# Attention and feed-forward on one core: partition sums split over two steps, and the softmax reciprocal placed behind the next maximum

## The chip, the cores and the metric

The kernel runs on one core of one Trainium2 chip. The metric is the device time of one execution in microseconds (us). The times shown are medians of several executions. One further execution was recorded with the hardware profiler; all times inside the kernel come from that one.

## What is computed

The reference is an attention with mixing across heads, followed by a feed-forward layer. Cut to what matters:

```
B, H, S, D = 4, 12, 448, 64
scores = (q @ k^T) / sqrt(D)                  # per batch and head
scores = einsum('bhij,hg->bgij', scores, w_pre)
attn   = softmax(scores, axis=-1)
attn   = einsum('bhij,hg->bgij', attn, w_post)
x      = (attn @ v) as [B*S, 768]
h      = x @ w_in                             # 768 -> 2048
out    = (h * sigmoid(1.702 h)) @ w_out       # 2048 -> 768
```

## The kernel before

**Steps.** Attention is cut into 180 steps: four batches, and 45 groups of ten query rows (the last has eight) in each. Ten rows by twelve heads make 120 partitions, so one step's scores are a tile of 120x448. The main loop runs over the step `i`, and what it emits is, engine by engine, the order in which the engines work; no scheduler reorders it. In step `i` it emits, in this order:

- the gather of the scores of step `i+4` from HBM (SyncE's queue, SP), into one of four buffers `r`;
- `mix(i+1)` on TensorE: the product with the first mixing matrix, into one of two PSUM buffers `mx`;
- for batch 0, `post_whole(i-2)` (the second mixing) and `keep_whole(i-3)`; for the later batches `keep_upper(i-4)` on ScalarE;
- for batch 0, `weigh_mix(i-1)` on GpSimd; for the later batches `weigh(i-1)` (GpSimd, writes `w`), `upper(i-1)` (ScalarE, writes `a`), `lower(i-1)` (GpSimd). All need the reciprocal `rs` of step `i-1`;
- `peak(i)` on VectorE (L286, the row maximum `nm`) and `expo(i)` on ScalarE (L293, the exponential `e` with its row sum `sm`, which frees the `mx` buffer). With `expo(i)` GpSimd turns the row sum into `rs` (L299);
- `run_jobs(i)`: the side jobs whose turn has come (below);
- products of the feed-forward layer (`h`, L588, and `po`, L627), 2.15 groups a step once the first batch has been through attention, `post(i-3)`, the scores of later chunks (`qk`) and the context products (`av`);
- last on VectorE, `keep_lower(i-4)` (L383) and `inverse(i)` (L304), the reciprocal of `rs`, in place.

After the last step only feed-forward products are left.

**Side jobs.** A job has a first step, the jobs that it comes after with a lag in steps, and a cost in the tokens of an engine; a job that isn't urgent waits until its engine's tokens suffice. The largest are sixteen conversions of weight slices (`convert`): fetch in three parts, five VectorE instructions a part (`w_f`, L484 to L504), a sum of squares on ScalarE (`waste`, L96), the sum over partitions and the scale, the upper part on ScalarE and the lower on VectorE (`w_p`, L532 and L537), and a store to HBM, from where the feed-forward stage fetches each slice again (`wt`). Other jobs scale q, k and v of the later batches (`tops`) and x (`gs`).

**Sums over partitions.** Each scale needs a sum over all partitions. `add_all` (L104 to L109) does it: TensorE multiplies the partial sums by a matrix of ones, into the last 16 columns of the PSUM bank `pp` that holds the newest second mixing, and VectorE adds along the row (L109). Both are emitted at the same place in the same step. There are 28 such sums: 16 for weights (`w_n`), eight for q, k and v (`tops`), four for x (`gs`).

Of the kernel before, what the change touches and what calls it, by code (L numbers as in the profile page):

```python
# [38 lines left out]
def attention_then_feed_forward(ctx, tc, q, k, v, w_pre, w_post, w_in, w_out, out):  # L39
# [63 lines left out]

    def add_all(m, parts):  # L104

        p, n = parts.shape
        t = last_pp[-1][:, 512 - 16:512 - 16 + n]
        nc.tensor.matmul(t, ones[:p, :], parts, start=True, stop=True)
        nc.vector.tensor_reduce(m, t, axis=AX.X, op=ALU.add)  # L109


# [26 lines left out]
    def top_of(name, b):  # L138
        i = 3 * b + "kqv".index(name)
        return tops[:, i:i + 1]  # L140

    def join(name, b):
        add_all(top_of(name, b), st["m" + name, b])

# [144 lines left out]
    def expo(i):  # L289
        K = rows_of(steps[i][1])[1] * H  # L290
        e = flow.tile([KG, S], F32, name=f"e_{i}", tag="e", bufs=3)
        sm = stat.tile([KG, 1], F32, name=f"sm_{i}", tag="sm")
        nc.scalar.activation(  # L293
            e[:K], row.pop(("mx", i))[:K, :S], AF.Exp, bias=row.pop(("nm", i))[:K, 0:1],
            scale=1.0, accum_out=sm[:K, 0:1],
        )
        rs = stat.tile([KG, 1], F32, name=f"rs_{i}", tag="rs")
        by = 2.0 ** -10 if steps[i][0] else 1.0
        nc.gpsimd.tensor_scalar(rs[:K], sm[:K], 1e-9, by, op0=ALU.add, op1=ALU.mult)  # L299
        row["e", i], row["rs", i] = e, rs  # L300

# [137 lines left out]

    def join_x(b):  # L440
        e = gs[:, b, 0:1]
        add_all(e, st["mx", b])

    def scale_x(b):
# [19 lines left out]
    def convert(kind, s, first):  # L464
# [45 lines left out]

        def join_w():
            t["n"] = stat.tile([128, 1], F32, name=f"{nm}_n", tag="wn")
            add_all(t["n"], t["m"])

# [31 lines left out]
        for a in range(NP):  # L546
# [11 lines left out]
            sizes.append(job(first, "A", 0.7, lambda a=a: size(a), after=[(last, 1)]))  # L558
        j = job(first, "D", 0.2, join_w, after=[(x, 1) for x in sizes])
        j = job(first, "D", 0.9, scale_w, after=[(j, 0)])  # L560
# [172 lines left out]
    for b in range(1, B):  # L733
# [6 lines left out]
        for name, first, ready in (("k", z - 25, z - 17), ("q", z - 23, z - 17), ("v", z - 8, z + LAG + 7)):  # L740
# [3 lines left out]
            for i in range(THIRDS):  # L744
# [3 lines left out]
                a["stage"][1].append(sq[-1])  # L748
            jn = job(0, "D", 0.2, lambda name=name, b=b: join(name, b), after=[(x, 1) for x in sq], urgent=True)
            sizes[name] = job(0, "D", 0.7, lambda name=name, b=b: scale(name, b), after=[jn], urgent=True)  # L750
            for i in range(THIRDS):
# [146 lines left out]
    sq = [job(1 + 2 * i, {"A": 1.6}, 0, lambda eng, i=i: squares("v", 0, i, eng, 2), urgent=True) for i in range(THIRDS)]  # L898
    j = job(1, "D", 0.2, lambda: join("v", 0), after=sq, urgent=True)
    job(1, "D", 0.9, lambda: scale("v", 0), after=[j], urgent=True)  # L900

# [50 lines left out]
    while quanta or i < N + LAG + 12:  # L952
# [15 lines left out]
        if GPB <= i - LAG - 1 < N:  # L968
            keep_upper(i - LAG - 1)
            spend("A", 0.55)  # L970
        if 0 <= i - 1 < GPB:
            weigh_mix(i - 1)
# [8 lines left out]
        if i < N:  # L981
            peak(i)
            spend("D", 0.62)
            expo(i)
            spend("A", 0.82)
        run_jobs(i)
# [13 lines left out]
        for b, c, pr in at_context.pop(i, []):  # L1000
# [7 lines left out]
            if c == NCH - 1 and pr == NPAIR - 1:  # L1008
                z = i
                a = job(z + 2, "D", 0.2, lambda b=b: join_x(b), urgent=True)  # L1010

                def finish(b=b, z=z):
                    scale_x(b)
                    x_done[b] = cur[0] + 1
                job(z + 3, "D", 0.9, finish, after=[a], urgent=True)
        slot()
# [3 lines left out]
        if GPB <= i - LAG - 1 < N:  # L1020
            keep_lower(i - LAG - 1)
            spend("D", 0.64)
        if i < N:
            inverse(i)
            spend("D", 0.15)
        owed = min(owed, 3.0)
# [44 lines left out]
```

## Time and profile before

| | us |
|---|---|
| median of 3 runs | 1029.36 |
| lowest and highest run | 1024.65, 1032.99 |
| the profiled execution | 1027.42 |
| its span in the profile | 1025.7 |

The span runs from the first to the last instruction that the profile shows; the profiled execution is 1.7 us longer than its span. Mean granted clock of TensorE over the execution: 0.961 of full speed. In the profile PE is TensorE, PEld its weight loads, DVE VectorE, ACT ScalarE, POOL GpSimd, and SP or SPq SyncE's queue of transfers. A wait is idle time of an engine, put down to the instruction that ended it.

### The profile page before, as it was taken

Reading aid. Unit: us, or ns where it says so; the run is one execution under the profiler, and the core shown is the slowest. Engines: PE = TensorE matmul, PEld = TensorE weight load, DVE = VectorE, ACT = ScalarE, POOL = GpSimd, SP = SyncE. Lnnn points to the kernel's source line nnn. Section 1 sums busy time; section 2 is a strip of 40 time slices with the busy share of each in tenths; the row PEclk is TensorE's granted clock in tenths of the full one; section 3 lists DMA queues with packets and bytes.
Section 4 is the critical chain, followed back from the end, with each engine's and each line's share of the span. In section 5 each row is a group of like instructions: output and inputs, shape, how many; then the busy total and the mean of one; then the engine's idle time right before and its main releaser. Section 6 shows DMA issues by size and latency. Waiting matters only on the chain.

```text
span 1025.7 us, 19868 instructions
## 1 busy us (share of the span) xinstructions
PE 925.0 (90%) x7344; PEld 542.4 (53%) x7344; DVE 628.8 (61%) x1389; ACT 605.2 (59%) x1380; POOL 354.5 (35%) x536
## 2 busy tenths in 40 slices
PE   5678878877899889999899999999899999999998
PEld 4345555544455444555455555656455666555554
DVE  5658786698976796554644575555645565443334
ACT  3666768677577676765657657656656564323332
POOL 0111111145433455343533454334534444001221
PEclk9888999888999998999999999999999999999999
DMA  8988979768557656654676647546654341234322
GB/s 301 289 275 313 332 267 323 259 197 245 190 198 244 232 187 181 192 172 131 202 225 207 202 150 234 166 130 179 212 164 146 108 148 64 93 123 151 118 93 85
DMA packets 66565, 198.19 MB, mean 193 GB/s; under 512 B 7668, under 2 KB 32372, under 8 KB 66468
## 3 DMA queue, kind: packets, MB, share of 16 engines
q1 hardware_dynamic: 66064, 196.83, 59.4%
q8 instruction: 58, 0.95, 0.4%
q14 instruction: 39, 0.32, 0.1%
q10 hardware_dynamic: 404, 0.09, 0.1%
HBM read 140.27 MB, written 56.62 MB: 192 GB/s over the span
## 4 chain that ended last, share of the span: by engine, by line
PE 62%; DVE 17%; ACT 8%; DMA 8%; issue 3%; POOL 1%; SPq 0%; ACTq 0%; DVEq 0%; POOLq 0%
PE po L627 19%; PE h L588 18%; PE mx L279 8%; PE av L408 4%; PE qk L243 3%; PE pp L356 2%; PE pp L358 2%; PE pp L357 2%; DVE w_p L537 2%; DMA sd<-sc 2%; ACT waste L96 2%; DVE w_f L504 2%; DMA w<-in_moe_w_out_dram 2%; DVE nm L286 2%; ACT e L293 1%
## 5 line engine op out<-in xcount | busy, mean ns | idle before, releaser
L627 PE MATMUL po<-g,wt 128*128 128x448 f16 x1152 | 243.8, 355 | 11.3 <-DVE th L609 6.8
L588 PE MATMUL h<-x,wt 128*128 128x448 f16 x1152 | 244.1, 356 | 3.9 <-ACT sc L253 2.9
L279 PE MATMUL mx<-r,wa 120*120 120x448 f32 x360 | 183.3, 592 | 40.0 <-ACT e L293 29.7
L343 POOL TENSOR_TENSOR a<-w,a 120x448 f16<-120x448 f32 x135 | 150.8, 1117 | 130.2 <-issue 71.5
L627 PEld LDWEIGHTS <-wt 128*128 128x128 f16 x1152 | 109.4, 99 | 130.0 <-issue 45.1
L588 PEld LDWEIGHTS <-wt 128*128 128x128 f16 x1152 | 109.2, 98 | 117.0 <-issue 31.2
L329 POOL TENSOR_SCALAR w<-e,rs 120x448 f32<-120x448 f32 x135 | 88.2, 653 | 227.3 <-DVE rs L304 217.8
L337 ACT ACTIVATE a<-e,rs 120x448 f16<-120x448 f32 x135 | 91.0, 674 | 106.1 <-DVE rs L304 106.1
L657 DVE SCALAR_TENSOR_TENSOR acc<-po,ct,acc 128x448 f32<-128x448 f32 x141 | 96.1, 682 | 74.3 <-PE po L627 72.2
L293 ACT ACTIVATE e<-mx,nm 120x448 f32<-120x448 f32 x180 | 113.6, 631 | 31.2 <-POOL wr L309 25.4
L609 DVE SCALAR_TENSOR_TENSOR th<-th,h 128x448 f32<-128x448 f32 x64 | 39.7, 620 | 137.8 <-ACT th L606 137.8
L606 ACT ACTIVATE th<-h,ct 128x448 f32<-128x448 f32 x64 | 40.5, 633 | 140.2 <-PE h L588 129.6
L253 ACT COPY sc<-qk 120x448 f32<-120x448 f32 (+1 forms) x186 | 89.6, 532 | 41.8 <-PE qk L233 28.9
L286 DVE TENSOR_REDUCE nm<-mx 120x1 f32<-120x448 f32 x180 | 108.9, 605 | 1.9 <-PE mx L279 1.9
L356 PE MATMUL pp<-wp,a 120*112 120x120 f16 x540 | 95.7, 220 | 14.8 <-DVE p L383 14.3
L279 PEld LDWEIGHTS mx<-r,wa 120*120 120x120 f32 x360 | 61.6, 193 | 83.9 <-ACT e L293 47.0
L299 POOL TENSOR_SCALAR rs<-sm 120x1 f32<-120x1 f32 x180 | 56.8, 315 | 115.8 <-ACT e L293 103.8
L358 PE MATMUL pp<-wp,a 120*112 120x120 f16 x540 | 95.1, 219 | 0.0
L357 PE MATMUL pp<-wp,a 120*112 120x120 f16 x540 | 94.9, 218 | 0.0
L383 DVE TENSOR_TENSOR p<-pp,p 112x480 f16<-112x480 f32 x135 | 87.2, 647 | 5.9 <-ACT p L379 5.9
L356 PEld LDWEIGHTS <-a 120*112 120x112 f16 x540 | 71.5, 132 | 26.9 <-DVE p L383 12.1
L357 PEld LDWEIGHTS <-a 120*112 120x112 f16 x540 | 71.8, 133 | 15.9 <-issue 9.5
(126 smaller groups left out, 1258.1 us busy)
## 6 DMA issues: line engine op xcount, KB each, us to landing
wt<-wd SPq DMA_DIRECT2D x64, 768.0 KB
r<-sd SPq DMA_DIRECT2D x176, 210.0 KB
sd<-sc SPq DMA_DIRECT2D x72, 420.0 KB
w<-in_moe_w_in_dram SPq DMA_DIRECT2D x24, 512.0 KB
w<-in_moe_w_out_dram SPq DMA_DIRECT2D x24, 512.0 KB
wd<-w_p SPq DMA_DIRECT2D x16, 768.0 KB
sd<-sc SPq DMA_DIRECT2D x24, 308.0 KB
out_dram<-acc SPq DMA_DIRECT2D x24, 224.0 KB
```

Source lines behind the costliest of these rows:

```text
L253: (nc.scalar.copy if engs[x] == "A" else nc.vector.tensor_copy)(t[:n, x, :], two[x][:n, :S])
L279: nc.tensor.matmul(mx[:K, :S], st["wa", b][:K, :K], row.pop(("r", i))[:K, :], start=True, stop=True)
L286: nc.vector.tensor_reduce(nm[:K], row["mx", i][:K, :S], axis=AX.X, op=ALU.max, negate=True)
L293: nc.scalar.activation(e[:K], row.pop(("mx", i))[:K, :S], AF.Exp, bias=row.pop(("nm", i))[:K, 0:1], scale=1.0, accum_out=sm[:K, 0:1],)
L337: nc.scalar.activation(a1[:K], row.pop(("e", i))[:K], AF.Copy, scale=row.pop(("rs", i))[:K, 0:1])
L343: nc.gpsimd.tensor_tensor(a2[:K], row.pop(("w", i))[:K], row["a1", i][:K], op=ALU.subtract)
L356: nc.tensor.matmul(o, a1[:K, js], wp1[:K, :, :n], start=True, stop=False)
L357: nc.tensor.matmul(o, a1[:K, js], wp2[:K, :, :n], start=False, stop=False)
L358: nc.tensor.matmul(o, a2[:K, js], wp1[:K, :, :n], start=False, stop=True)
L588: nc.tensor.matmul(h, w[:, i, c, fc * 128:(fc + 1) * 128], x[:, j, c, :], start=(n == 0), stop=(n == len(terms) - 1),)
L627: nc.tensor.matmul(po, w[:, j, fc, e * 128:(e + 1) * 128], g[:, i, fc, :], start=(n == 0), stop=(n == len(terms) - 1),)
L657: nc.vector.scalar_tensor_tensor(a, po, c, a, op0=ALU.mult, op1=ALU.add)
```

## The change

Two things are moved. First, the sums: `add_all` becomes `add_over` (TensorE's product) and `add_along` (VectorE's addition), emitted by two jobs, the second one step after the first. Both are urgent, where the weights' sum was not. The job that uses the sum now runs in the same step as the addition. Second, the reciprocal: `inverse(i)` goes from the end of step `i` to step `i+1`, right behind `peak(i+1)`. For that `peak(i)` and `expo(i)` go ahead of `weigh(i-1)`, `upper(i-1)` and `lower(i-1)`, and GpSimd's `rs` becomes a function of its own (`shifted`), emitted behind `lower(i-1)` as before.

```diff
-    def add_all(m, parts):
+    def add_over(parts):
 
         p, n = parts.shape
         t = last_pp[-1][:, 512 - 16:512 - 16 + n]
         nc.tensor.matmul(t, ones[:p, :], parts, start=True, stop=True)
+        return t
+
+    def add_along(m, t):
         nc.vector.tensor_reduce(m, t, axis=AX.X, op=ALU.add)
 
+    def sum_jobs(first, m, parts, after):
+
+        t = {}
+
+        def over():
+            t["t"] = add_over(parts())
+
+        j = job(first, None, 0, over, after=after, urgent=True)
+        return job(first, "D", 0.2, lambda: add_along(m(), t["t"]), after=[j], urgent=True)
...
-        j = job(first, "D", 0.2, join_w, after=[(x, 1) for x in sizes])
+        j = sum_jobs(first, total, lambda: t["m"], [(x, 1) for x in sizes])
         j = job(first, "D", 0.9, scale_w, after=[(j, 0)])
...
+        if i < N:
+            peak(i)
+            spend("D", 0.62)
+        if 0 <= i - 1 < N:
+            inverse(i - 1)
+            spend("D", 0.15)
+        if i < N:
+            expo(i)
+            spend("A", 0.82)
         if 0 <= i - 1 < GPB:
             weigh_mix(i - 1)
             spend("G", 0.35)
...
             lower(i - 1)
             spend("G", 1.07)
         if i < N:
-            peak(i)
-            spend("D", 0.62)
-            expo(i)
-            spend("A", 0.82)
+            shifted(i)
         run_jobs(i)
...
             keep_lower(i - LAG - 1)
             spend("D", 0.64)
-        if i < N:
-            inverse(i)
-            spend("D", 0.15)
```

The same is done for the sums of q, k, v and x.

**VectorE, steps 35 and 36, before.** `nm` is the maximum, `rs` the reciprocal, `w_n` the sum of a weight slice, and the short rows behind it the scale.

```order
L286 TENSOR_REDUCE nm_1638<-mx_1587 120x1
L109 TENSOR_REDUCE w_3_n<-pp_1630 128x1
L81 TENSOR_SCALAR w_3_n<-w_3_n 128x1
L82 TENSOR_SCALAR ew<-w_3_n 128x1
L518 TENSOR_SCALAR ew<-ew 128x1
L520 RECIPROCAL w_3_s<-ew 128x1
L521 TENSOR_SCALAR w_3_s<-w_3_s 128x1
L523 TENSOR_SCALAR ew<-ew 128x1
L304 RECIPROCAL rs_1643<-rs_1643 120x1
L286 TENSOR_REDUCE nm_1676<-mx_1628 120x1
```

The addition stands right behind the maximum of its step, and the reciprocal of the step ahead of the next maximum. The same steps in the changed kernel:

```order
L296 TENSOR_REDUCE nm_1609<-mx_1561 120x1
L319 RECIPROCAL rs_1577<-rs_1577 120x1
L112 TENSOR_REDUCE w_3_n<-pp_1563 128x1
L81 TENSOR_SCALAR w_3_n<-w_3_n 128x1
L82 TENSOR_SCALAR ew<-w_3_n 128x1
L529 TENSOR_SCALAR ew<-ew 128x1
L531 RECIPROCAL w_3_s<-ew 128x1
L532 TENSOR_SCALAR w_3_s<-w_3_s 128x1
L296 TENSOR_REDUCE nm_1645<-mx_1601 120x1
L319 RECIPROCAL rs_1617<-rs_1617 120x1
```

The reciprocal behind a maximum is now that of the step before it, and the addition reads a bank that TensorE filled a step earlier. The slice is also another one, of the first weight matrix and not of the second: the conversions have fallen behind by this place.

**VectorE in step 88, before.** `tops`, `ev` and `s_v` are the scale of v, `p` is `keep_lower`.

```order
L286 TENSOR_REDUCE nm_5150<-mx_5051 120x1
L81 TENSOR_SCALAR tops<-tops 128x1
L82 TENSOR_SCALAR ev_5157<-tops 128x1
L151 RECIPROCAL s_v_5158<-ev_5157 128x1
L152 TENSOR_SCALAR s_v_5158<-s_v_5158 128x1
L153 TENSOR_SCALAR ev_5157<-ev_5157 128x1
L156 TENSOR_SCALAR ex<-ev_5157,e_wp 128x1
L383 TENSOR_TENSOR p_3_4882<-pp_5077,p_3_4882 112x48x10
L304 RECIPROCAL rs_5155<-rs_5155 120x1
```

All conversions are over here (the last store stands in step 83). The same step in the changed kernel, from the last instruction of that scale on:

```order
L166 TENSOR_SCALAR ex<-ev_5133,e_wp 128x1
L548 SCALAR_TENSOR_TENSOR w_7_p<-w_7_f_4220,w_7_s,w_7_p 128x512
L548 SCALAR_TENSOR_TENSOR w_7_p<-w_7_f_4318,w_7_s,w_7_p 128x512
L548 SCALAR_TENSOR_TENSOR w_7_p<-w_7_f_4628,w_7_s,w_7_p 128x512
L495 TENSOR_SCALAR w_7_f_5146<-w_7_64_2_4705 128x512
L499 TENSOR_SCALAR w_7_f_5146<-w_7_f_5146 128x512
L398 TENSOR_TENSOR p_3_4844<-pp_5052,p_3_4844 112x48x10
```

Conversion work stands here that was done earlier before; the last store now stands in step 95.

**ScalarE, steps 70 and 71, before.** `e` is the exponential, `a` is `upper`, `p` is `keep_upper`.

```order
L379 CAST p_1_2936<-pp_3726 112x48x10
L337 ACTIVATE a_70_3767<-e_3704,rs_3707 120x448
L293 ACTIVATE e_3773,sm_3774<-mx_3693,nm_3771 120x448
L96 ACTIVATE waste,mq_3641<-qa_2_3646 128x448 x2
L532 ACTIVATE w_6_p<-w_6_f_2953,w_6_s 128x512
```

The upper part of step 70 stands ahead of the exponential of step 71. In the changed kernel:

```order
L394 CAST p_1_2874<-pp_3665 112x48x10
L303 ACTIVATE e_3706,sm_3707<-mx_3628,nm_3703 120x448
L352 ACTIVATE a_70_3711<-e_3634,rs_3643 120x448
L96 ACTIVATE waste,mq_3572<-qa_2_3577 128x448 x2
L96 ACTIVATE waste,w_6_m<-w_6_f_3437 128x512
```

The exponential now stands ahead of the upper part.

## Rows read from the trace of the kernel before

**Rows 1.** Busy time by stage; columns as its first line says, instructions in brackets.

```profile
core 0: us, PE busy (x) PEld busy (x) DVE busy (x) ACT busy (x) POOL busy (x), PEclk, DMA share, GB/s
34.00:195.00 161.00, 129.29 (x803) 81.16 (x802) 119.82 (x311) 117.35 (x299) 29.89 (x90) 0.92 0.88 299
195.00:258.00 63.00, 47.74 (x345) 28.75 (x345) 50.12 (x112) 40.89 (x95) 27.04 (x39) 0.83 0.70 215
258.00:414.00 156.00, 136.72 (x1073) 76.65 (x1073) 119.57 (x242) 107.62 (x243) 68.82 (x85) 0.95 0.65 212
414.00:472.00 58.00, 58.00 (x559) 34.86 (x557) 31.81 (x74) 37.80 (x88) 23.70 (x36) 1.00 0.53 160
472.00:870.00 398.00, 383.32 (x3523) 229.29 (x3521) 225.97 (x483) 245.82 (x558) 178.94 (x257) 1.00 0.54 168
```

**Rows 2.** Waits from 34 to 195 us: us in total, times, longest us.

```profile
ACT e L293 <- POOL wr L309: 25.4, 19, 3.2
PE mx L279 <- ACT e L293: 19.9, 15, 5.2
DVE rs L304 <- POOL rs L299: 17.1, 15, 3.3
DVE w_n L109 <- PE pp L108: 15.1, 8, 4.7
...
PE av L397 <- DVE x L431: 9.3, 3, 4.6
```

**Rows 3.** Timeline, parts of steps 34 to 37: start, us, instruction, in brackets the idle time before it.

```profile
158.01 0.16 DVE L304 RECIPROCAL rs<-rs 120x1 f32<-120x1 f32 x1 [0.76 <-POOL rs L299]
158.09 0.60 DVE L286 TENSOR_REDUCE nm<-mx 120x1 f32<-120x448 f32 x1
...
158.66 1.01 PE L279 MATMUL mx<-r,wa 120*120 120x448 f32 x2
...
160.65 0.16 DVE L109 TENSOR_REDUCE w_n<-pp 128x1 f32<-128x3 f32 x1 [1.95 <-PE pp L108]
...
160.89 0.65 ACT L293 ACTIVATE e<-mx,nm 120x448 f32<-120x448 f32 x1
...
166.59 0.60 DVE L286 TENSOR_REDUCE nm<-mx 120x1 f32<-120x448 f32 x1
...
167.29 0.64 ACT L293 ACTIVATE e<-mx,nm 120x448 f32<-120x448 f32 x1 [0.48 <-POOL wr L309]
```

**Rows 4.** Waits from 195 to 258 us.

```profile
DVE w_n L109 <- PE pp L108: 6.5, 3, 5.2
...
DVE rs L304 <- POOL rs L299: 3.2, 3, 1.4
```

**Rows 5.** Waits from 258 to 414 us.

```profile
DVE tops L109 <- PE pp L108: 6.8, 2, 3.4
...
DVE rs L304 <- POOL rs L299: 4.7, 5, 1.4
```

**Rows 6.** Waits from 472 to 870 us.

```profile
ACT a L337 <- DVE rs L304: 70.2, 48, 3.8
...
DVE rs L304 <- POOL rs L299: 33.7, 35, 1.4
```

**Rows 7.** Conversion instructions (tile w_f, which w_p reads): columns DVE busy, ACT busy.

```profile
0.00:1026.00 1026.00, 175.10 (x288) 65.59 (x144) 0.96 0.60 193
```

**Rows 8.** The maxima (L286), one a step, in two stretches: column DVE busy.

```profile
257.90:414.50 156.60, 15.71 (x26) 0.95 0.65 212
414.50:471.90 57.40, 7.25 (x12) 1.00 0.53 159
```

**Rows 9.** Chain of waits from 30 to 290 us: start, us, link.

```profile
49.80 9.79 DMA wd<-w_p
...
105.53 7.47 DMA r<-sd
```

**Rows 10.** A wait of the whole span.

```profile
PE pp L108 <- ACT p L379: 6.5, 7, 2.6
```

More of the change, by code (lines that the diff above doesn't have):

```diff
@@ L140, in top_of @@
         return tops[:, i:i + 1]
-    def join(name, b):
-        add_all(top_of(name, b), st["m" + name, b])
     def scale(name, b):
@@ L296, in expo, with shifted @@
         )
+        row["e", i], row["sm", i] = e, sm
+    def shifted(i):
+        K = rows_of(steps[i][1])[1] * H
+        sm = row.pop(("sm", i))
         rs = stat.tile([KG, 1], F32, name=f"rs_{i}", tag="rs")
@@ L299, in expo @@
         nc.gpsimd.tensor_scalar(rs[:K], sm[:K], 1e-9, by, op0=ALU.add, op1=ALU.mult)
-        row["e", i], row["rs", i] = e, rs
+        row["rs", i] = rs
     def inverse(i):
@@ L438, in x_size @@
                    st["mx", b][:, 2 * c + half:2 * c + half + 1], "A")
-    def join_x(b):
-        e = gs[:, b, 0:1]
-        add_all(e, st["mx", b])
     def scale_x(b):
@@ L509, in size, with total @@
             square_sum(t["f", a].bitcast(F32), t["m"][:, a:a + 1], "A")
-        def join_w():
+        def total():
             t["n"] = stat.tile([128, 1], F32, name=f"{nm}_n", tag="wn")
-            add_all(t["n"], t["m"])
+            return t["n"]
         def scale_w():
@@ L748, in attention_then_feed_forward @@
                 a["stage"][1].append(sq[-1])
-            jn = job(0, "D", 0.2, lambda name=name, b=b: join(name, b), after=[(x, 1) for x in sq], urgent=True)
-            sizes[name] = job(0, "D", 0.7, lambda name=name, b=b: scale(name, b), after=[jn], urgent=True)
+            jn = sum_jobs(0, lambda name=name, b=b: top_of(name, b), lambda name=name, b=b: st["m" + name, b], sq)
+            sizes[name] = job(0, "D", 0.7, lambda name=name, b=b: scale(name, b), after=[(jn, 0)], urgent=True)
             for i in range(THIRDS):
@@ L898, in attention_then_feed_forward @@
     sq = [job(1 + 2 * i, {"A": 1.6}, 0, lambda eng, i=i: squares("v", 0, i, eng, 2), urgent=True) for i in range(THIRDS)]
-    j = job(1, "D", 0.2, lambda: join("v", 0), after=sq, urgent=True)
-    job(1, "D", 0.9, lambda: scale("v", 0), after=[j], urgent=True)
+    j = sum_jobs(1, lambda: top_of("v", 0), lambda: st["mv", 0], sq)
+    job(1, "D", 0.9, lambda: scale("v", 0), after=[(j, 0)], urgent=True)
     at_scores = {}
@@ L1009, in attention_then_feed_forward @@
                 z = i
-                a = job(z + 2, "D", 0.2, lambda b=b: join_x(b), urgent=True)
+                a = sum_jobs(z + 2, lambda b=b: gs[:, b, 0:1], lambda b=b: st["mx", b], [])
                 def finish(b=b, z=z):
@@ L1014, in finish @@
                     x_done[b] = cur[0] + 1
-                job(z + 3, "D", 0.9, finish, after=[a], urgent=True)
+                job(z + 3, "D", 0.9, finish, after=[(a, 0)], urgent=True)
         slot()
```

## The prediction

> **What bounds the kernel now.** First the busy time by stage [rows 1], cut at the places where the kind of work changes: batch 0 (34 to 195 us, steps 0 to 44), batch 1 before any feed-forward product (to 258, steps 45 to 57), feed-forward beside conversions (to 414, steps 58 to 83), feed-forward without conversions (to 472, and on to 870); behind them the tail. From 414 on PE is the bound: busy for 58.00 of 58 and 383.32 of 398 us, and the tail is feed-forward products alone. Ahead of that it is not: it is idle for 31.7 us of the first stage (161 less 129.29), 15.3 of the second, 19.3 of the third, 66.3 in all. PE does the same products in both kernels, and the last of them end the span, so a gain is idle time of PE that goes, or a higher clock.
>
> Next, who lets PE wait in the first stage [rows 2]. 19.9 us are mixings (L279) that wait for an exponential to free a `mx` buffer, 9.3 are context products that wait for a VectorE instruction on x: 29.2 of the 31.7. The exponential in turn stood 19 times, 25.4 us in all, behind something; the row names GpSimd's `wr`, but the exponential of step 37 starts at 167.29, 0.10 us after its own maximum ends (166.59 + 0.60) [rows 3], so VectorE is what it waits for. VectorE is busy for 119.82 of 161 us, and its 41.2 us of idle time are mostly two waits: 17.1 us in 15 reciprocals that wait for GpSimd's `rs`, and 15.1 us in eight additions that wait for TensorE's product of ones. Both are waits at the head of an in-order queue. The timeline shows one of each [rows 3]: the reciprocal of step 34 waits 0.76 us and the next maximum stands behind it; 2.5 us later the addition waits 1.95 us. These are the waits that the change takes aim at.
>
> **The change, part by part.** The number of steps, the feed-forward groups in each step and the products are unchanged; nothing is added but order. PE's 28 products of ones stay where a sum is due, VectorE's additions follow a step later.
>
> *Reciprocal.* Moved behind the next maximum, `inverse(i-1)` needs an `rs` that GpSimd made most of a step earlier; a step is some 3.6 us (161 / 45), the waits were at most 3.3. I count all of them as gone from VectorE: 17.1 us in the first stage, 3.2 in the second [rows 4], 4.7 in the third [rows 5]. In return each maximum now stands ahead of the reciprocal, so `upper` and `weigh` of the step before start about 0.6 us later (a maximum takes 0.60 [rows 3]). Behind them come `lower` and, three steps on, `post`; that distance is the cover, and I cost it at nothing. Were the cover gone, 48 waits for the reciprocal in 472 to 870 [rows 6] would each be 0.6 us longer, 29 us of ScalarE, which is idle there for 152 us (398 less 245.82).
>
> *Additions.* A step after its product the addition finds it done: 15.1, 6.5 and 6.8 us go. What is late next is the maximum: it needs `mix`, which needs the exponential two steps back. Step 36's mixing runs from 158.66 to 159.67 us [rows 3], so with the addition's wait gone the next maximum could start at about 159.7, ahead of where the addition now begins (160.65); but its exponential still follows one that began at 160.89, though that one's maximum was done at 158.69: there ScalarE itself was behind. So a wait that goes is not a microsecond won each time.
>
> The sum now lies a step longer in a PSUM bank that the mixing two steps later wants. VectorE adds next behind the reciprocal, PE reaches that mixing only after the following exponential (0.65 us) and mixing (1.01 us) [rows 3]: 1.7 us of cover, cost nothing. Without it the nearest row is the opposite wait, 15.1 us in eight cases, 1.9 us each; at most ten sums of the first stage could cost that, 19 us. In the trace a product of ones waited for ScalarE's reading of the same bank seven times, 6.5 us [rows 10]. The Trainium skill (PSUM — Partial Sum Buffer, section "PSUM bank collisions raise a hardware error") says that accesses of two engines to one bank have to be kept apart by semaphores, whichever columns they touch; the trace agrees with it in those seven waits. By that rule alone this term would be a loss between 0 and the 19 us above.
>
> *Conversions.* One more step lies between a conversion's product and its scale, so each conversion takes longer and the next begins later: the last store moves from step 83 to step 95. Counted in the order, VectorE has 12 `w_f` and 3 `w_p` instructions fewer in steps 0 to 44, 5 `w_f` fewer in 45 to 57, 7 `w_f` more and 3 `w_p` fewer in 58 to 83, and 10 `w_f` and 6 `w_p` more in 84 to 95. One takes 0.61 us (175.10 / 288 [rows 7], both kinds together). That is 9.1 us less VectorE work in the first stage (15 instructions), 3.0 less in the second (5), 2.4 more in the third (4), 9.7 more in 414 to 472 (16). The fetches and stores on SP's queue move with them; the tightest is weight slice 7, stored in step 89, fetched back from step 90, used from step 93 (before: 78, 86, 93). Stores and fetches of the trace took up to 9.8 us [rows 9], and a step there is 4.8 (57.40 / 12 [rows 8]), so about 19 us for two transfers: just enough.
>
> *The sum.* First stage: VectorE loses 17.1 + 15.1 + 9.1 = 41.3 us of waits and work. Nothing of it on the path gives 0, and PE can't win more than the 29.2 us that it waits for others. ScalarE is busy for 73% (117.35 / 161), PE for 80%, the transfers for 88% of the time, so the four take turns at the end of a wait; I take a third, 14 us. Second: 3.2 + 6.5 + 3.0 = 12.7, bounds 0 and 12.7; here VectorE at 80% (50.12 / 63) is the fullest engine, so half, 6 us. Third: 4.7 + 6.8 - 2.4 = 9.1, bounds -2.4 and 9.1; I take 4 us, a bit under half, because PE's idle time there (19.3 us) has other causes too. 414 to 472: 9.7 us of work go where VectorE is idle for 26.2 (58 less 31.81), bounds: nothing lost; or the 12 steps run at the pace of the stage with conversions, 6.02 us a step (156.60 / 26) against 4.78 [rows 8], 14.9 lost. I take 4, since the added work a step (9.7 / 12 = 0.8 us) is about half of what that stage carries (65 conversion instructions in 26 steps, 1.5 us a step) and there is idle time to take it. 472 to 870: VectorE's 33.7 us of waits for `rs` go [rows 6], but PE is at work for 96%; bounds 14.7 (its idle time) and 0, I take 0. Tail: PE alone, 0. Together 14 + 6 + 4 - 4 = 20 us off the profiled execution: 1027.4 - 20 = 1007.4. That execution lies 1.9 us under the median of the runs shown, 1029.4.
>
> **The rivals.** *VectorE alone paced the early stages.* For: its idle time in the first stage is nearly all of the two kinds that go. Then PE's 29.2 us, the second stage's 12.7 and the third's 9.1 are won, 4 lost: 47.0 off, 980.4. A higher clock would help too: it was granted at 0.83 in the second stage and 1.00 from 414 on. Against: ScalarE and the transfers are nearly as full.
>
> *The gain is hidden anyway.* The chain of waits from 30 to 290 us passes through transfers, a store of 9.79 us and a gather of 7.47 among them [rows 9], and in 34 to 195 us they are busy for 0.88 of the time at 299 GB/s. If they or ScalarE set the pace, the first stage wins 3 us, the second 3, the third 0, and 2 are lost behind: 4 off, 1023.4. Against: no wait of PE in [rows 2] ends with a transfer. The Trainium skill (DMA: Bandwidth & Descriptors, section "Where 436 GB/s comes from") puts the memory's limit for one core at about 358 GB/s; by that limit (an estimate from that page) the stage's bytes would need 134 us, so that page would allow a gain of 27 us and no more.
>
> *The moved conversions starve PE (slower).* Place: steps 84 to 95, where PE has no idle time. If VectorE, with conversions back in its queue, is late for the maxima and the gates there, these 12 steps run at 6.02 us: +14.9, and with nothing won ahead, 1042.3. It decides from the point where the early stages win less than these steps lose. For: 41.5 of 58 us (31.81 + 9.7) is 72%, near the 77% (119.57 / 156) at which PE lost 19.3 us in the stage before. Against: those early stages have real waits that go.
>
> That the change doesn't do what it says (the waits stay) would need `rs` to come a whole step late; it belongs to the second rival.
>
> **How the numbers follow.** A measurement of this kernel tells about 1% from no change, 1019.1 to 1039.7. My forecast, 1007.4 with its own range of 994 to 1019, gets 0.52; the larger gain (980.4) 0.14; the hidden gain (1023.4) 0.22; the slower one (1042.3) 0.12. Faster by over 1%: 0.52 + 0.14 = 0.66; within 1%: 0.22; slower: 0.12. The range from 985 to 1033 leaves out some 0.08 of the larger gain and the slower case's 0.12.
>
> **What would show it.** Right: waits of VectorE for `rs` and for the product of ones near zero; 34 to 195 us shortened by some 14 us, the next stage by 6; steps 84 to 95 longer by a few us; 84 later steps unchanged. Wrong: VectorE's idle time in the first stage as large as before, under the name of the maximum waiting for `mix` (PE or ScalarE then set the pace); PE waits for `wt` of slice 7 around step 93; or mixings that wait for an addition in their bank.

## The result and the profile after

The changed kernel takes 1036.79 us (median of 10 runs, 1032.85 to 1039.14) where the kernel before takes 1029.86 (10 runs, 1024.65 to 1033.23): a ratio of 1.0073, 95% interval 1.005 to 1.0096. It is a little slower, where 20 us less was forecast. The profiled execution took 1032.85 us, the lowest of the ten; its span is 1031.1 us, 5.4 more than before.

The start of the maximum of a step, read from the timeline, divides both kernels at the same step. The table is worked out from these starts; the lower rows are experiments that follow.

```
us from step to step   0-44   45-57  58-83  84-95  96-178  rest
before                 196.6   61.3  156.6   57.4  392.2  161.6
after                  187.6   57.7  161.0   67.2  394.7  162.9
e1_recip_only          198.5   63.3  161.0   57.4  396.2  162.9
e2_sums_only           193.6   56.9  159.6   68.1  394.5  161.5
e3_weights_one_step    199.8   62.8  159.3   57.7  394.4  162.9
e4_cadence             199.9   59.4  155.8   57.7  393.2  162.9
e5_sums_on_time        201.4   57.6  156.4   57.7  392.8  161.6
e6_rs_ahead            198.8   57.3  155.1   57.7  393.0  163.2
e7_late_only           192.2   57.8  160.3   66.2  390.5  161.6
e8_recip_rs_ahead      199.3   61.0  158.6   57.4  393.7  163.2
e9_old_place_rs_ahead  201.7   57.9  150.9   58.0  393.9  162.4
e10_no_least           191.4   57.3  151.0   57.4  390.5  161.5
e11_more_bytes         206.5   61.4  156.7   57.4  389.7  161.7
e12_after_rs_ahead     187.1   55.0  159.5   66.8  389.2  162.9
```

"0-44" runs from the start of the span. The change wins 9.0 and 3.6 us ahead of step 58, and gives back 4.4, 9.8, 2.5 and 1.3 behind it. The 1.3 comes from the boundary chosen: from the maximum of step 178 instead of 179 on, the rest is 164.0 us before and 164.1 after. Each row is one profiled execution, and executions of one kernel lie over 8 us apart (1024.65 to 1033.23). In 96-178 the kernel before differs by 1.7 to 2.5 us from e7, e10 and e11, whose code is the same there, so differences of that size in this table mean nothing by themselves.

The products of TensorE are the same in all these kernels, so a stretch gets longer in one of two ways: TensorE idles more, or it is busy longer. The next table separates them: idle time of PE between the same steps (a stretch less its PE busy time; the first from 34 us on), the sum, PE's busy time from 34 us to step 178, the granted clock there as a share of full speed (a mean over stretches at full and at half speed), and the granted clock of whole executions, in the mean of all runs of that kernel.

```
PE idle, us            34us-44 45-57 58-83 84-95 96-177  sum   busy  clock  all runs
before                  31.7   15.2   19.3   0.0   14.7  80.9  746.8  0.960  0.962
after                   26.0   13.8   25.7   5.3   16.1  87.0  746.0  0.963  0.960
e1_recip_only           34.1   15.9   21.6   0.0   15.9  87.5  753.8  0.953  0.954
e2_sums_only            28.4   14.7   25.2   5.0   14.5  87.8  748.5  0.963  0.963
e3_weights_one_step     34.0   19.3   20.0   0.1   16.0  89.4  749.5  0.957  0.957
e4_cadence              30.6   17.1   18.1   0.1   16.2  82.1  748.8  0.961  0.958
e5_sums_on_time         32.0   14.2   15.6   0.1   14.5  76.4  753.0  0.954  0.959
e6_rs_ahead             29.8   15.1   17.0   0.1   14.5  76.5  750.1  0.957  0.960
e7_late_only            26.7   11.3   25.7   4.5   14.7  82.9  747.7  0.963  0.959
e8_recip_rs_ahead       29.6   16.1   17.9   0.0   14.1  77.7  757.2  0.949  0.953
e9_old_place_rs_ahead   31.2   14.0   16.3   0.1   14.5  76.2  750.4  0.957  0.962
e10_no_least            26.3   14.0   16.2   0.0   14.7  71.2  740.0  0.970  0.971
e11_more_bytes          37.2   15.1   19.4   0.0   13.9  85.6  749.6  0.954  0.960
e12_after_rs_ahead      26.9   11.1   24.9   5.0   14.0  81.9  740.5  0.974  0.964
```

The changed kernel idles 6.1 us more than before and is busy as long. Where the code is the same, idle time repeats within 1 us (before and e11 from step 45 on), so it tells more than the times of the first table. Busy time goes with the granted clock: 740.5 us at 0.974 in e12, 757.2 at 0.949 in e8. Why one kernel is granted less than another no run shows.

Busy time by stage of the changed kernel, between the same steps. It answers to [rows 1], and its first line names the columns.

```profile
core 0: us, PE busy (x) PEld busy (x) DVE busy (x) ACT busy (x) POOL busy (x), PEclk, DMA share, GB/s
34.00:187.60 153.60, 127.58 (x805) 79.72 (x805) 113.85 (x292) 112.32 (x288) 33.60 (x89) 0.94 0.91 304
187.60:245.30 57.70, 43.85 (x333) 26.91 (x333) 45.66 (x100) 40.20 (x96) 29.05 (x39) 0.80 0.71 216
245.30:406.20 160.90, 135.17 (x1075) 75.25 (x1075) 124.14 (x246) 105.12 (x239) 79.85 (x88) 0.97 0.66 212
406.20:473.40 67.20, 61.89 (x568) 36.59 (x567) 43.81 (x99) 46.00 (x107) 28.68 (x39) 0.98 0.51 158
```

VectorE's idle time in the first stage is 153.6 - 113.85 = 39.8 us, against 41.2 before: no less, though two kinds of waits were to go from it. What it now waits for (us in total, times, longest us), from 34 to 187.6 us, to be read against [rows 2]:

```profile
DVE w_n L112 <- ACT p L390: 12.3, 5, 3.1
DVE nm L296 <- PE mx L289: 10.3, 9, 2.9
DVE rs L319 <- POOL rs L314: 7.8, 9, 2.0
DVE tops L112 <- ACT p L390: 3.2, 1, 3.2
```

The additions (L112) waited 15.1 us for TensorE's product; now they wait 12.3 + 3.2 = 15.5 us in six cases for a ScalarE copy. The reciprocals (L319) still wait 7.8 of 17.1 us, and 10.3 us of waits of the maximum (L296) for the mixing are new. In the last attention stage, 473.4 to 868.2 us, the waits for `rs` have grown from the 33.7 us of [rows 6]:

```profile
DVE rs L319 <- POOL rs L314: 41.8, 35, 2.0
```

Why the addition waits, in the timeline of the changed kernel (start, us, instruction, idle time before it):

```profile
147.39 0.98 PE L334 MATMUL pp<-wr,e 120*112 120x120 f32 x8
...
148.21 0.29 PE L108 MATMUL pp<-w_m,ones 128*128 128x3 f32 x2
...
150.38 0.95 ACT L263 COPY sc<-qk 120x448 f32<-120x448 f32 x2
...
151.22 0.58 ACT L390 COPY p<-pp 112x480 f32<-112x480 f32 x1
...
151.83 0.16 DVE L112 TENSOR_REDUCE w_n<-pp 128x1 f32<-128x3 f32 x1 [2.87 <-ACT p L390]
```

The product of ones (L108) is done at 148.5, in the bank that holds the second mixing of 147.39. A step later `keep_whole` (L390) copies that mixing out of the bank, and the order puts it ahead of the addition. ScalarE comes to it at 151.22, behind copies of scores, and only as it ends does the addition, which reads other columns of the bank, begin. The Trainium skill (PSUM — Partial Sum Buffer, section "PSUM bank collisions raise a hardware error") has accesses of two engines to one bank kept apart, a read by ScalarE against a read by VectorE included; the trace agrees, in these six waits of 15.5 us.

Why the reciprocal waits, in the same view, steps 112 and 113:

```profile
556.01 0.61 DVE L296 TENSOR_REDUCE nm<-mx 120x1 f32<-120x448 f32 x1
...
556.72 0.63 ACT L303 ACTIVATE e<-mx,nm 120x448 f32<-120x448 f32 x1 [0.80 <-DVE rs L319]
...
557.25 0.19 ACT L303 ACTIVATION_READ_ACCUMULATOR e<-mx,nm 120x1 f32 x1
557.34 0.66 ACT L352 ACTIVATE a<-e,rs 120x448 f16<-120x448 f32 x1
...
558.13 1.04 POOL L358 TENSOR_TENSOR a<-w,a 120x448 f16<-120x448 f32 x1 [0.71 <-POOL w L344]
...
559.26 0.19 POOL L314 TENSOR_SCALAR rs<-sm 120x1 f32<-120x1 f32 x1
...
559.49 0.16 DVE L319 RECIPROCAL rs<-rs 120x1 f32<-120x1 f32 x1 [1.71 <-POOL rs L314]
```

The exponential's row sum is read out by 557.44. `rs` could be made then, but GpSimd has `lower` (L358) of the step before first in its queue, and `lower` needs `upper` (L352), which now stands behind the exponential on ScalarE. So `rs` starts 1.9 us after the exponential's end. Over steps 96 to 178 the mean from the exponential's end to the end of `rs` is 2.30 us, against 1.10 before.

### The profile page after: what moved, and what is told of

Same layout as the page of the kernel before. It is cut to its first block, busy times and chain, and to the rows that moved or that the text cites. A ratio compares the mean times of both kernels' runs of the same rounds, so it can differ in the third digit from the quotient of the medians.

```text
span 1031.1 us, 19788 instructions
## 1 busy us (share of the span) xinstructions
PE 925.2 (90%) x7344; PEld 540.1 (52%) x7344; DVE 639.4 (62%) x1386; ACT 605.2 (59%) x1383; POOL 377.0 (37%) x542
## 4 chain that ended last, share of the span: by engine, by line
PE 57%; DVE 23%; ACT 12%; issue 4%; DMA 3%; POOL 1%; SPq 0%; ACTq 0%; DVEq 0%; POOLq 0%
PE po L638 18%; PE h L599 17%; PE mx L289 7%; PE av L423 4%; DVE nm L296 3%; DVE w_p L548 2%; DVE w_f L503 2%; ACT waste L96 2%; ACT e L303 2%; PE qk L253 2%; ACT sc L263 2%; PE pp L371 2%; DVE p L398 2%; DVE w_f L499 2%; DVE w_f L509 2%
## 5 line engine op out<-in xcount | busy, mean ns | idle before, releaser
L638 PE MATMUL po<-g,wt 128*128 128x448 f16 x1152 | 248.0, 359 | 18.7 <-ACT sc L263 9.3
L303 ACT ACTIVATE e<-mx,nm 120x448 f32<-120x448 f32 x180 | 115.7, 643 | 149.2 <-DVE rs L319 143.6
L358 POOL TENSOR_TENSOR a<-w,a 120x448 f16<-120x448 f32 x135 | 149.1, 1104 | 133.0 <-issue 64.4
L344 POOL TENSOR_SCALAR w<-e,rs 120x448 f32<-120x448 f32 x135 | 112.4, 832 | 217.5 <-DVE rs L319 108.3
L668 DVE SCALAR_TENSOR_TENSOR acc<-po,ct,acc 128x448 f32<-128x448 f32 x135 | 91.9, 681 | 79.1 <-PE po L638 77.4
L296 DVE TENSOR_REDUCE nm<-mx 120x1 f32<-120x448 f32 x180 | 110.6, 615 | 13.0 <-PE mx L289 12.7
L352 ACT ACTIVATE a<-e,rs 120x448 f16<-120x448 f32 x135 | 89.9, 666 | 5.1 <-DVE rs L319 5.0
L371 PEld LDWEIGHTS <-a 120*112 120x112 f16 x540 | 71.3, 132 | 36.5 <-DVE p L398 9.6
L665 POOL TENSOR_TENSOR acc<-acc,pt 128x448 f32<-128x448 f32 x33 | 38.3, 1165 | 124.6 <-ACT pt L662 124.0
L314 POOL TENSOR_SCALAR rs<-sm 120x1 f32<-120x1 f32 x180 | 44.4, 247 | 105.8 <-ACT e L303 93.1
```

The lines of the kernel that those rows point to most:

```text
L296: nc.vector.tensor_reduce(nm[:K], row["mx", i][:K, :S], axis=AX.X, op=ALU.max, negate=True)
L303: nc.scalar.activation(e[:K], row.pop(("mx", i))[:K, :S], AF.Exp, bias=row.pop(("nm", i))[:K, 0:1], scale=1.0, accum_out=sm[:K, 0:1],)
L344: nc.gpsimd.tensor_scalar(w[:K], e[:K], row["rs", i][:K, 0:1], 1.0, op0=ALU.mult, op1=ALU.mult)
L358: nc.gpsimd.tensor_tensor(a2[:K], row.pop(("w", i))[:K], row["a1", i][:K], op=ALU.subtract)
L371: nc.tensor.matmul(o, a1[:K, js], wp1[:K, :, :n], start=True, stop=False)
L638: nc.tensor.matmul(po, w[:, j, fc, e * 128:(e + 1) * 128], g[:, i, fc, :], start=(n == 0), stop=(n == len(terms) - 1),)
```

## The experiments

Each was compared with the kernel before on the same chip, whose medians were 1028.6 to 1029.8 us. The chip was not the same for all experiments; from one to the next, the ratios compare best.

**e1, the reciprocal part alone.** The kernel before with these lines of the change and no other.

```diff
+        if i < N:
+            peak(i)
...
+        if 0 <= i - 1 < N:
+            inverse(i - 1)
...
+        if i < N:
+            expo(i)
...
-            peak(i)
...
-            expo(i)
...
+            shifted(i)
...
-        if i < N:
-            inverse(i)
```

> The reciprocal behind the next maximum alone; all sums in one step as before, so the conversions keep the schedule of before (last store in step 83). If the lateness of the conversions is what costs and the removed waits were worth something, this is faster than before by 5 to 10 us (1020 to 1025). If the early gain of the changed kernel was only conversion work moved out of the first stages, it equals before (1028 to 1032). If the new order itself costs behind step 96 (upper part behind the exponential, GpSimd's chain longer), it is slower than before by 3 to 6 us (1033 to 1036).

Measured: 1041.55 us, ratio 1.0126 (1.0099 to 1.0152). The part alone costs 12 us, more than any of the three theories had it; waits for `rs` over the whole span are 65.4 us, against 63.0 before. The conversions keep their schedule (last store in step 83), and neither the early gain nor the loss in 84-95 appears. The loss is spread over all other stages. By the second table it is 6.6 us of idle time of PE and 7.0 of longer busy time, at a lower clock (0.954 in the mean of all runs, 0.962 before).

**e2, the sums part alone.** `sum_jobs` in place of `add_all`, the reciprocal as before.

> The sums over two steps alone; the reciprocal stays at the end of its step. The conversions are late as in the changed kernel (last store in step 95). If their lateness costs, this is slower than before by 5 to 10 us (1035 to 1040), with steps 84 to 95 some 10 us longer. If the reciprocal's order is what costs, it is within 3 us of before.

Measured: 1034.89 us, 1.0049 (1.0031 to 1.0067), at the fast end of the expected loss. The early gain and the loss of 10.7 us in 84-95 are both here, and here the last store is in step 95: they belong to the sums part.

**e3, the changed kernel with the weights' sums in one step again.**

```diff
-        j = sum_jobs(first, total, lambda: t["m"], [(x, 1) for x in sizes])
+        def join_w():
+            t_ = add_over(t["m"])
+            add_along(total(), t_)
+
+        j = job(first, "D", 0.2, join_w, after=[(x, 1) for x in sizes])
```

> The changed kernel with the weights' sixteen sums in one step again; q, k, v and x keep two steps, the reciprocal stays moved. Conversions on the schedule of before. Lateness theory: steps 84 to 95 return to 57 us, total 1020 to 1026. Moved work theory: the first stages lose their 12 us again, total 1028 to 1032. Reciprocal theory: 1033 to 1036.

Measured: 1039.81 us, 1.0098 (1.007 to 1.0126). That is slower than each of the three theories had it. Conversions are back on schedule; the gain and the loss in 84-95 are both gone (57.7 us), so of the sums it is the weights' that move them. What is left is about the cost of e1, whose reciprocal part this kernel keeps.

**e4, the changed kernel with the conversions on schedule, sums split.**

```diff
-            up = job(first, "A", 0.72, lambda a=a: w_upper(a, "A"), after=[(j, 1)] + [(x, 0) for x in stores[-1:]])
+            up = job(first, "A", 0.72, lambda a=a: w_upper(a, "A"), after=[(j, 0)] + [(x, 0) for x in stores[-1:]])
```

> The changed kernel, but the upper part of a converted slice is emitted in the step of its scale and not a step later, so that the conversions keep the schedule of before (last store in step 83) though their sums take two steps. Lateness theory: 1018 to 1026, faster than before by what the additions' waits were worth. Moved work theory: 1028 to 1032. If ScalarE now waits for the scale on VectorE at the upper part, 16 such waits of 1 to 2 us: up to 1040.

Measured: 1032.45 us, 1.0029 (1.0013 to 1.0044). This is just slower than the moved-work theory had it. Sums and reciprocal stand as in the changed kernel, and steps 0-44 win nothing (199.9 against 196.6; PE idles 30.6 us there, against 31.7). VectorE waits for the mixing instead, from 34 to 195 us:

```profile
DVE nm L296 <- PE mx L289: 14.0, 11, 3.6
```

**e5, sums split and on schedule, the reciprocal in its old place.** e2 with the edit of e4.

> The sums part alone, with the conversions kept on the schedule of the kernel before (the upper half of a weight may follow its scale in the same step, so the last store falls in step 83 as before); the reciprocal stays in its old place. Theory that late conversions price the sums: the sums part alone took 1034.9, its steps 84 to 95 cost 10 us; with them back at 57.4 us and steps 0 to 57 no longer won, about 1026 to 1031, and steps 84 to 95 within 1 us of the kernel before. Theory that the addition costs by itself (it now stands behind ScalarE's copies that read the same bank): 1034 or more on this schedule too.

Measured: 1029.28 us, 0.9993 (0.9976 to 1.0009). In time the split wins nothing and loses nothing; what e2 lost comes only with late conversions. PE idles 4.5 us less than before, none of it in the first stage, but is busy longer, at a lower clock, so the split may be worth those 4.5 us; the time doesn't show it.

**e6, e4 with `rs` ahead of `lower`.**

```diff
-            lower(i - 1)
-            spend("G", 1.07)
         if i < N:
             shifted(i)
+        if GPB <= i - 1 < N:
+            lower(i - 1)
+            spend("G", 1.07)
```

> The changed kernel with conversions on schedule (1032.5) and one more edit: GpSimd makes rs of a step ahead of lower of the step before, so it no longer stands behind an instruction that waits for ScalarE's upper. Theory that the reciprocal waits because rs stands behind lower: in steps from 45 on VectorE's waits for rs fall from 68.6 us over the span to under 40, the mean from a maximum's start to its reciprocal's end falls from 6.3 to about 5.2 us, and the time to 1021 to 1028. Theory that the reciprocal's place behind the maximum is what costs, by the 0.6 us that upper and weigh start later: no change from 1032.5, within 3 us.

Measured: 1026.63 us, 0.997 (0.9959 to 0.9981), faster than both kernels and 5.8 us under e4. From the exponential's end to that of `rs` it is 0.56 us instead of 2.30 in steps 96 to 178; over the span 9.4 us of waits for `rs` are left of 68.6. From the maximum's start to the reciprocal's end it is 5.46 us in steps 96 to 178, 6.00 in e4; about 5.2 was expected. In the last attention stage the wait did not vanish, it changed its name; e6 from 472 to 862 us, where [rows 6] had 33.7 us for `rs`, and e4 50.2 from step 84 on:

```profile
DVE th L620 <- ACT th L617: 73.2, 27, 6.0
DVE acc L668 <- PE po L638: 46.4, 45, 2.5
```

The same wait of `th` was 43.4 us in the changed kernel: 30 us more of it stand in the place of the 42 for `rs`, and the stage is as long as before (393.0 against 392.2 us), as PE is the bound there. Of the 4.0 us between the profiles of e6 and e4, 3.2 lie in 0-57.

**e7, late conversions alone.** The kernel before with a step more ahead of each weight's sum.

```diff
-        j = job(first, "D", 0.2, join_w, after=[(x, 1) for x in sizes])
+        j = job(first, "D", 0.2, join_w, after=[(x, 2) for x in sizes], urgent=True)
```

> The kernel before with nothing changed but a step more between the sizes of a weight and their sum, so that the conversions run as late as in the changed kernel (the last store in step 95); product of ones and addition stand together as before, and so does the reciprocal. Theory that the moved conversions are the price: steps 84 to 95 take 67 us where the kernel before takes 57.4, steps 0 to 57 win 8 to 13 us all the same, and the time is 1030 to 1036, as the sums part alone (1034.9). Rival, that the early gain comes from the waits removed: steps 0 to 57 win under 4 us, steps 84 to 95 still lose 10, 1036 to 1041.

Measured: 1031.05 us, 1.0014 (0.9994 to 1.0034), as expected but not clear of the kernel before. The first table shows the pattern of the changed kernel without any of its edits to waits: 7.9 us won ahead of step 58, just under the expected 8 to 13, 3.7 lost in 58-83 and 8.8 in 84-95. By itself the lateness costs 2.0 us of idle time of PE: 8.9 less ahead of step 58, 10.9 more in 58-95. Busy time in 84-95, where PE now idles for 4.5 us and did not before:

```profile
410.30:476.50 66.20, 61.73 (x568) 36.42 (x567) 42.65 (x100) 46.16 (x107) 29.16 (x39) 0.98 0.53 162
```

That this is the conversions' work is seen in the chain of waits of the changed kernel, here from 427 to 442 us (start, us, link):

```profile
427.58 1.84 ACT w_p L543 x3
429.42 0.61 ACT waste L96 x2
430.03 0.84 ACT sc L263 x2
430.87 0.38 ACT x L440
...
431.27 0.53 DVE x L446
431.81 0.59 DVE acc L668
432.40 0.56 DVE p L398
432.96 0.53 DVE nm L296
...
434.61 2.85 DVE w_p L548 x3
...
439.78 1.02 DVE w_f L509
...
440.82 0.69 DVE w_f L515
```

VectorE is busy for only 65% of 406.2 to 473.4 us (43.81 / 67.2), yet the chain goes through 1.84 us of `w_p` on ScalarE, then 2.85 us of `w_p` and 1.71 of `w_f` on VectorE, with the step's maximum and the feed-forward's `acc` in one queue with them.

**e8, e1 with `rs` ahead of `lower`** (the edit of e6).

> The reciprocal part alone (1041.6), with rs of a step made ahead of lower of the step before on GpSimd. Theory that rs stands behind lower: most of the 12 us over the kernel before go, 1028 to 1034, and VectorE's waits for rs in 472 us to the end of the steps fall from about 45 to under 20 us. Theory that the later start of upper and weigh costs: 1039 to 1043, as without the edit.

Measured: 1036.61 us, 1.0069 (1.0049 to 1.0089). The waits for `rs` go in the later batches (1.6 us from step 84 on), but only 5 of the 12 us come back, fewer than expected: neither theory holds alone. Of the waiting all came back: PE idles 9.8 us less than in e1. What is left is busy time: PE idles 77.7 us, less than the 80.9 before, and is busy 10.4 us longer, at the lowest clock of all these kernels (0.953 in the mean of all runs, 0.961 for the kernel before on that chip). Whether the reciprocal's new place lowers the clock, and why e6, which has it too, is granted more, stays open. The additions, not split here, do wait longer than in [rows 2], from 34 to 195 us in e8:

```profile
DVE w_n L109 <- PE pp L108: 20.1, 8, 5.1
DVE nm L286 <- PE mx L279: 6.5, 5, 1.7
DVE rs L309 <- POOL rs L304: 5.4, 9, 1.4
```

But PE idles no longer for it in that stage (29.6 us, 31.7 before).

**e9, e5 with `rs` ahead of `lower`, the reciprocal in its old place.**

> Sums split and conversions on schedule, the reciprocal in its old place at the end of its own step (that alone took 1029.3), and rs of a step made ahead of lower of the step before. It differs from the best kernel so far (1026.6) in the reciprocal's place alone. Theory that the reciprocal's place behind the next maximum is worth nothing once rs comes in time: 1025 to 1028, waits for rs under 25 us of VectorE over the span where the kernel before has 63. Theory that the place is what wins: 1029 to 1031.

Measured: 1026.25 us, 0.9972 (0.9954 to 0.999), the same as e6. With `rs` in time, the reciprocal's place behind the next maximum is worth nothing. The waits for `rs` are 58.5 us, not the under 25 expected, and the time is as good as with 9.4: they bound nothing. The 3.0 us under e5 are at the edge of what the intervals tell apart, and PE idles as long in both (76.2 and 76.4 us).

**e10, less VectorE work.** The kernel before without one instruction of each part of a conversion; the job and its place stay.

```diff
         def least(a):
-            f = t["f", a].bitcast(F32)
-            nc.vector.tensor_scalar_max(f, f, TINY)
+            pass
```

> The kernel before without the maximum with a tiny number in each weight's conversion (48 VectorE instructions of 0.43 us left out, their place in the schedule kept; that step of the conversion is not computed). Steps 0 to 44 lose 24 or 25 of them, 10.6 us of VectorE work and no transfer. Theory that VectorE's work paces the early steps, as the gain of the late conversions suggests: steps 0 to 44 take 5 to 10 us less, steps 45 to 83 another 2 to 6, and the time is 1016 to 1023. Theory that the transfers do, which the late conversions also move out of these steps: steps 0 to 44 within 2 us, and 1026 to 1030.

Measured: 1012.64 us, 0.9842 (0.9812 to 0.9871), faster than the expected 1016 to 1023. In steps 0-44 10.2 us of work less (24 instructions; six more stand ahead of step 0) bring 5.2 us; in 45-83 18 instructions less, 8.5 us, bring 4.0 + 5.6 = 9.6. Of idle time of PE it is 5.4 us in the first stage and 4.3 in 45-83, about half of the work in both; the other 5.3 us in 45-83 are shorter busy time of PE, at a higher clock (0.971 in the mean of all runs). Work is worth something where waits were worth next to nothing. Each conversion also has one instruction less to go through, which this run doesn't tell apart from the work.

**e11, more transfers.**

```diff
+        if i < GPB and i % 2:
+            more_bytes(i)
...
+    def more_bytes(i):
+        nc.sync.dma_start(out=spare[i], in_=w_in[0][:, :WN // 6].bitcast(I32))
```

> The kernel before with 22 more transfers of 262 KB, one in every second step of 0 to 44 on SP's queue, from the weights in memory to a spare place in memory (nothing waits for them): 5.8 MB on top of the 48 MB that the stage moves. Theory that transfers pace the early steps: steps 0 to 44 take 10 to 20 us more. Theory that VectorE's work does: under 3 us more, 1028 to 1034.

Measured: 1035.41 us, 1.006 (1.0037 to 1.0082). Steps 0-44 take 9.9 us more, just under the expected 10 to 20; 5.5 us of it are idle time of PE, the rest longer busy time at a lower clock. At the 299 GB/s of [rows 1] the 5.8 MB take 19.3 us, so transfers cost about half of their length here, as VectorE's work does in e10: neither paces the stage alone. The queue of SP has 22 more entries as well, which this run doesn't tell apart. From 34 us to the start of step 45 in e11:

```profile
34.00:206.50 172.50, 135.26 (x807) 85.15 (x807) 120.81 (x312) 117.60 (x299) 30.65 (x90) 0.89 0.91 312
```

**e12, the changed kernel with `rs` ahead of `lower`** and nothing else, conversions late.

> The changed kernel (1036.8) with the one edit that rs of a step is made ahead of lower of the step before; the conversions stay late. On schedule the same edit took 1032.5 to 1026.6. Theory of two separate side effects (late conversions about 4 us, rs behind lower about 6): 1030 to 1032, steps 84 to 95 still 66 to 68 us, waits for rs under 15 us over the span. Rival, that one hides the other: 1026 to 1028, or 1035 and more.

Measured: 1028.69 us, 0.9993 (0.9966 to 1.0019), 8.1 under the changed kernel and a little better than expected; its runs spread from 1021.83 to 1034.19, so the step to e6 (1026.63) is uncertain, and its profiled execution (1022.24) is one of the fastest. 84-95 still take 66.8 us.

The four kernels with both edits to the waits are then

```
us (idle us of PE)      rs behind lower        rs ahead of lower
conversions late        1036.8 (87.0, after)   1028.7 (81.9, e12)
conversions on time     1032.5 (82.1, e4)      1026.6 (76.5, e6)
```

In idle time of PE the two side effects add up: `rs` behind `lower` costs 5.1 and 5.6 us, the late conversions 4.9 and 5.4.

## Why the prediction was wrong

**What bounds the kernel** was read rightly behind step 83: removing some 48 us of waits for `rs` from there on (e4 to e6, 50.2 to 1.7) changes next to nothing (96-178 take 393.2 and 393.0 us), as the sum had it for 472 to 870 us. For the first stage the prediction left open what paces it and took a third of 41.3 us. That sum mixed two things with different worth. Of the 41.3 us, 9.1 were work moved away; e10 suggests that work there is worth about half, and e7, which moves just that work and its transfers, wins 4.4 us. The other 32.2 us were waits, and no kernel that touches only them on the old schedule wins in this stage (e1, e4, e5, e6 and e9 take 198.5 to 201.7 us, against 196.6). PE's idle time says the same: 30.6 us in e4, 32.0 in e5, 29.8 in e6, against 31.7. The 9.0 us that the changed kernel does win there look like a smaller version of the forecast 14, but 5.7 of them are idle time that goes, of which e7 has 5.0 without any edit to the waits; the other 3.3 are shorter busy time of PE. The changed kernel wins 4.6 us more than e7, and 3.9 of these are busy time, 127.6 us against 131.5 with the clock granted at 0.94 and 0.92. The stage in e7:

```profile
34.00:192.20 158.20, 131.51 (x804) 83.00 (x804) 112.37 (x293) 113.32 (x288) 29.05 (x89) 0.92 0.88 295
```

In the same way e4, e5, e6 and e9 are busy some 4 to 6 us longer there than the kernel before and idle no longer. Whether the edits bring about these clocks or the one profiled execution of each does, stays open.

**The step on the reciprocal failed.** It said that `inverse(i-1)` needs an `rs` that GpSimd made most of a step earlier, and counted all its waits as gone. They are 66.7 us over the span, against 63.0; in the first stage, which has no `upper` and `lower`, more than half of them went, and behind step 83 they grew from 38.1 to 47.4. The time at which `rs` is made moved with the edit: putting the exponential ahead of `upper` on ScalarE delays `lower`, and `rs` stands behind `lower` in GpSimd's queue. The order of both engines showed this beforehand; the prediction looked only at VectorE's queue, and at the step's length. What the later start of `upper` and `weigh`, which it costed at nothing, has to do with it was not tried by itself. e6 and e12 show the price of `rs` behind `lower`: 5.8 and 8.1 us, of which 5.6 and 5.1 are idle time of PE.

**The step on the additions failed** in its first sentence: "A step after its product the addition finds it done". It does, and still waits 15.5 us, for ScalarE's copy out of the same bank. The prediction weighed that rule for the mixing two steps later, where it saw 1.7 us of cover and gave up to 19 us otherwise; the reader that came between was missed. The cover it spoke of was nearly enough: TensorE's second mixing waited for an addition in its bank for 8.0 us in five cases of the whole span of the changed kernel, none of them in the first stage, where up to 19 were allowed for:

```profile
PE pp L371 <- DVE gs L112: 4.5, 3, 3.3
...
PE pp L371 <- DVE tops L112: 1.9, 1, 1.9
PE pp L371 <- DVE w_n L112: 1.6, 1, 1.6
```

In time the split on schedule is worth nothing (e5, 0.9993); in idle time of PE it may be worth 4.5 us, none of them in the first stage.

**The moved conversions**: the term for 414 to 472 us was mis-sized, 4 us where 9.8 came (8.8 in e7), within its bound of 14.9; and 58-83, forecast as 4 us won, lost 4.4, most of it by the late conversions too (3.7 in e7). The place and the mechanism are those of the slower rival, and so is its deciding point: the three stages ahead win 9.0 + 3.6 - 4.4 = 8.2 us together, less than the 9.8 that these steps lose. With the steps at 67.2 / 12 = 5.60 us it stopped short of the 6.02 that the rival took. Putting the conversions back on schedule takes 4.3 us off (e4).

**The cases.** The rival that had the gain hidden anyway, 1023.4, was right that the waits taken away in the first stage win next to nothing. It was wrong in taking transfers or ScalarE as the only pace: VectorE's work counts as well (e10). The measured 1036.8 lies 3.8 us above the range and within 1% of the kernel before; two side effects took it there, the late conversions and `rs` behind `lower`: each alone undone takes 4.3 (e4) and 8.1 us (e12) off, both together 10.2 (e6). The forecast's own marks of a failure were the right ones: VectorE's idle time in the first stage is as large as before, partly under the maximum that waits for `mix`.

## What to carry to other kernels

A wait at the head of an in-order queue is worth its length only if nothing else is late with it; here 32 us of waits in one stage changed their names or came back and brought next to nothing, while work taken off the same engine brought about half of its length in idle time of PE. Separate idle time from busy time before reading a stage: here several us of the differences were busy time at another clock. When a consumer is moved, follow its producer through every queue in the new order (here ScalarE, then GpSimd), and look for any other reader of the bank that lies between the two. When one more step of lag is put in a chain of jobs, ask first where its work ends up: in a stage where PE was the bound, some 10 us of added VectorE work cost 9 to 11 us.

## What was not expected of the hardware

The same GpSimd instruction, `weigh`, slowed down in the changed kernel; columns of the page: line, engine, operation, names, shapes, count, busy us, mean ns, idle time before.

```profile
L344 POOL TENSOR_SCALAR w<-e,rs 120x448 f32<-120x448 f32 x135 | 112.4, 832 | 217.5 <-DVE rs L319 108.3
```

In the kernel before the mean is 653 ns (88.2 us in all), in e2 and e9, with the reciprocal in its old place, 656 both. The median does not change (639 and 642 ns); 34 of 135 take over 0.8 us, 2 before. One of them, in the timeline of the changed kernel:

```profile
597.78 0.15 DVE L319 RECIPROCAL rs<-rs 120x1 f32<-120x1 f32 x1
...
597.85 3.56 DVE L211 SCALAR_TENSOR_TENSOR kp<-kb,s_k,kp 128x896 f16<-128x896 f32 x3
...
598.03 2.44 POOL L344 TENSOR_SCALAR w<-e,rs 120x448 f32<-120x448 f32 x1 [2.86 <-DVE rs L319]
...
600.55 1.75 POOL L358 TENSOR_TENSOR a<-w,a 120x448 f16<-120x448 f32 x1
```

The reciprocal releases `weigh` in the same moment as VectorE goes on to a job's instruction with two inputs from SBUF, and `weigh` takes 2.44 us in place of 0.64, `lower` 1.75 in place of 1.04. In its old place at the end of the step the reciprocal was followed by the next maximum, which reads PSUM (as in [rows 3]). The Trainium skill (SBUF — State Buffer, section "Who interferes with whom") says that a VectorE instruction with two SBUF inputs contends with a GpSimd instruction that reads SBUF; these rows agree: 33 of the 34 over 0.8 us overlap such an instruction on a large tile, and of the 101 others two, which take 0.74 us. These 34 are 25 us of GpSimd time beyond 0.64 us each. Whether they cost the kernel anything was not tried by itself: e6 has 25 of them and takes the same time as e9, which has six.
